# A transformer prompt kernel: the start-up sequence of the first token group rearranged, and a bias vector loaded late and element by element

## The chip, the cores and the metric

The kernel runs on one core of a Trainium2 chip. The metric is device time in microseconds (us). The profile's span runs from the first to the last instruction, and it is 1.7 to 2.2 us shorter than the time.

The core's engines go by the profile's names. PE does the matmuls and the transposes, and PEld is its loading of weights. DVE, ACT and POOL do the element-wise work. SP issues the DMAs; those that POOL issues are called software DMAs here. A DMA has landed when the trace shows that all its data has arrived. A *front* is the work before the first matmul on real weights.

## The reference

The input x has 2048 rows of 1024 columns, in bf16. Two layers are applied, with the same weights each time. Each layer does this:

```python
x = x + A(layernorm(x), wqkv, wo)          # 32 heads; each token attends to 8 tokens, 2 apart, to its left
x = x + B(layernorm(x), w1, b1, w2, b2)    # gelu_tanh(h @ w1 + b1) @ w2 + b2, 3584 hidden columns
```

In A, the logits of tokens before the start of the sequence get -1e9.

## The kernel before

The rows are worked on in four groups of 512 per layer. For each group PE computes Q, K and V, later the output projection (`gen_wo`), and then the two feed-forward products. DVE, ACT and POOL do all else beside it.

**The first loads.** SP issues all weight and x loads in one order. The first Q weight `wq` comes in four pieces of 512 KB, mixed with the first four x tiles of 256 KB each:

```python
load_x(0, 0, 2)
for k in range(0, KD, 2):
    load_wq_piece(wq_first[k // (KD // 2)], k)
    if k < 4:
        load_x(0, 2 + k // 2, 3 + k // 2)
```

The order is x0, x1, wq0, x2, wq1, x3, wq2, wq3. After these come x4 to x11 and then `wk`.

**The front.** Two token tiles are normalized and transposed on PE (cuts marked):

```python
xn0 = norm(0)
xn1 = norm(1)
transpose_on_pe(xn0, xa[0][:, 0, :, :], parts=[act.copy] * 4)
ps = transpose_bias()                      # b1, loaded as 28 rows by a software DMA on POOL
transpose_on_pe(xn1, xa[0][:, 1, :, :], parts=[vec.tensor_copy] * 2 + [act.copy] * 2)
warm_up(2)                                 # two matmuls that nobody reads
act.copy(b1T[:], ps[:])
# ... statistics of tiles 2 and 3
```

**The Q phase of group 0.** (K(0), or key(0), is the K phase after it.) The first products use those two tiles only. They run in four quarters over the contraction, one for each `wq` piece: 7 chunks x 2 matmuls of 128x256, so 14 matmuls a quarter:

```python
for kq in range(4 if n == 0 else 0):
    for c in range(7):
        first[c] = qkv_chunk(wq, c, xnT, first.get(c), kq * (KD // 4), (kq + 1) * (KD // 4), 0, 2)
        # at (2, 3) and (3, 4): transposes of token tiles 2 and 3
```

**The output projection.** It has two weight tiles. Chunks 0 to 3 use the first tile and chunks 4 to 7 the second:

```python
for tt in range(NTT):
    for dh in range(2):
        for c in range(NCH):
            mm(ps[:], lhsT=oT[:, c, tt * P:(tt + 1) * P], rhs=wts[c // 4][:, c % 4, ...], ...)
```

Of the kernel before, what the change touches and what calls it, by code (L numbers as in the profile page):

```python
# [9 lines left out]
ALU = mybir.AluOpType  # L10
# [7 lines left out]
def kernel(  # L18
# [134 lines left out]
    make_identity(nc, ident[:])  # L153
    mask = const.tile([P, W - 1, HALO], F32, name="mask")
    khalo = const.tile([P, NCH, HALO], BF16, name="khalo")
    vhalo = const.tile([P, NCH, HALO], BF16, name="vhalo")
    zhalo = const.tile([P, NCH, HALO], BF16, name="zhalo")
    b1T = const.tile([P, KF], F32, name="b1T")
    b2bc = const.tile([P, D], BF16, name="b2bc")
    mv_ahead = const.tile([P, NTT, 2], F32, name="mv_ahead")  # L160
    rstd_ahead = const.tile([P, NTT, 1], F32, name="rstd_ahead")

    def build_constants():
        pool.memset(zhalo[:], 0.0)
        pool.memset(mask[:], 0.0)
        first = smp.tile([H, W - 1, HALO], F32, name="z")
        pool.memset(first[:], 0.0)
        for w in range(W - 1):
            pool.memset(first[:, w, 0:HALO - DIL * w], -1e9)
        pool.dma_start(mask[0::NTT, :, :], first[:])  # L170

    b1_rows = attp.tile([KF, P], BF16, name="abc")

    pool.dma_start(b1_rows[:], B_b1.rearrange("(j p) -> j p", p=P))

    def load_b2():
        pool.dma_start(b2bc[:], B_b2.unsqueeze(0).to_broadcast([P, D]))

    def transpose_bias():
        ps = psum.tile([P, KF], BF16, name="acc", bufs=8)  # L180
        pe(nc.tensor.transpose(ps[:], b1_rows[:], ident[:KF, :KF]))  # L181
        return ps


    def ln_stats(t, mv=None, rstd=None):
        stats = lnp.tile([P, 2, 6], F32, name="stats")
# [7 lines left out]
        pool.tensor_tensor(out=rstd[:], in0=rstd[:], in1=mhalf[:], op=ALU.pow)  # L194
        return mv, rstd

    def ln_stats_ahead(g):
        junk = lnp.tile([P, D], BF16, name="xn", bufs=3)
        for tt in range(NTT):
            t, mean, var = g * NTT + tt, mv_ahead[:, tt, 0:1], mv_ahead[:, tt, 1:2]  # L200
            less = lnp.tile([P, 1], F32, name="less")
            act.activation(junk[:], x[t][:], ACT.Identity, scale=-1.0 / D, accum_out=less[:])
            act.activation(junk[:], x[t][:], ACT.Square, bias=less[:], accum_out=var)
            pool.tensor_scalar(out=mean, in0=less[:], scalar1=-1.0, scalar2=None, op0=ALU.mult)
            rstd = rstd_ahead[:, tt, :]
            pool.tensor_scalar(out=rstd, in0=var, scalar1=1.0 / D, scalar2=EPS, op0=ALU.mult, op1=ALU.add)
            pool.tensor_tensor(out=rstd, in0=rstd, in1=mhalf[:], op=ALU.pow)

    def ln_norm(t, mv, rstd, xn=None):
        if xn is None:  # L210
# [1 line left out]
        vec.tensor_scalar(out=xn[:], in0=x[t][:], scalar1=mv[:, 0:1], scalar2=rstd[:], op0=ALU.subtract, op1=ALU.mult)  # L212
        return xn

    def transpose_on_pe(xn, out, parts=None):
        pst = psum.tile([P, KD, P], BF16, name="acc", bufs=8)
        for k in range(KD):
            pe(nc.tensor.transpose(pst[:, k, :], xn[:, k * P:(k + 1) * P], ident[:]))  # L218
        parts = parts or [act.copy]
        n = KD // len(parts)  # L220
        for h, copy in enumerate(parts):
            copy(out[:, h * n:(h + 1) * n, :], pst[:, h * n:(h + 1) * n, :])

    last_transpose = [None]

# [7 lines left out]
    def ln_first():  # L233

        xa[0] = new_xnT()
        vec.on = act.on = True
        mvs = {}
        stds = {}

        def stats(tt):  # L240
            st6 = lnp.tile([P, 2, 6], F32, name="stats")
            for h in range(2):
                vec.bn_stats(st6[:, h, :], x[tt][:, h * HALF:(h + 1) * HALF])
            mvs[tt] = lnp.tile([P, 2], F32, name="mv")
            vec.bn_aggr(mvs[tt][:], st6[:])
            stds[tt] = lnp.tile([P, 1], F32, name="std")
            act.activation(stds[tt][:], mvs[tt][:, 1:2], ACT.Sqrt, bias=eps_t[:])

        def norm(tt):
            rstd = lnp.tile([P, 1], F32, name="rstd")  # L250
            vec.reciprocal(rstd[:], stds[tt][:])
            return ln_norm(tt, mvs[tt], rstd)

        stats(0)
        stats(1)
        xn0 = norm(0)
        xn1 = norm(1)
        transpose_on_pe(xn0, xa[0][:, 0, :, :], parts=[act.copy] * 4)
        ps = transpose_bias()
        transpose_on_pe(xn1, xa[0][:, 1, :, :], parts=[vec.tensor_copy] * 2 + [act.copy] * 2)  # L260
        warm_up(2)
        act.copy(b1T[:], ps[:])
        stats(2)
        stats(3)
        for tt in range(2, 4):
            first_late.append((norm(tt), xa[0][:, tt, :, :]))
        vec.on = act.on = False
        act.hold()
# [38 lines left out]
    def gen_qkv(n, defer=False, qk_pool=None, v_late=False, qk_next=None, v_first=False, mix=0):  # L307
        g = n % NG
        xnT = xa.pop(n)
        s = st[n]  # L310
        s["prods"] = []
        qk_pool = qk_pool or attp
        if v_first:
            wv = load_qkv(2)
        wq = wq_first if n == 0 else load_qkv(0)
        if not v_first:
            wk = load_qkv(1)

        def values():
            vT = attp.tile([P, NCH, HALO + T], BF16, name="vT", bufs=2)  # L320
            s["vT"] = vT
            act.on = n > 2
            act.copy(vT[:, :, 0:HALO], (zhalo if g == 0 else vhalo)[:])
            act.on = False
            for c in range(NCH):
                ps = qkv_chunk(wv, c, xnT)
                act.copy(vT[:, c, HALO:], ps[:])
                yield
            if g + 1 < NG:
                act.copy(vhalo[:], vT[:, :, T:T + HALO])  # L330

        if v_first:
            yield from values()
            wk = load_qkv(1)
        if n == 0:
            early_tiles = ln_early((1, None), (2, qk_next))
            for _ in range(NTT):
                next(early_tiles)
            wv = load_qkv(2)
            for _ in early_tiles:  # L340
                pass
            load_x(3)
        qT = qk_pool.tile([P, NCH, T], BF16, name="qT")
        first = {}
        for kq in range(4 if n == 0 else 0):
            for c in range(7):
                first[c] = qkv_chunk(wq, c, xnT, first.get(c), kq * (KD // 4), (kq + 1) * (KD // 4), 0, 2)
                if (kq, c) == (2, 3):
                    transpose_on_pe(*first_late.pop(0))
                if (kq, c) == (3, 4):  # L350
                    for done in range(2):
                        act.copy(qT[:, done, 0:2 * P], first[done][:, 0:2 * P])
                    transpose_on_pe(*first_late.pop(0))
                    act.hold()
        if n == 0:
            first[7] = qkv_chunk(wq, 7, xnT, t0=0, t1=2)
        for c in list(first)[2:]:
            act.copy(qT[:, c, 0:2 * P], first[c][:, 0:2 * P])
        kT = qk_pool.tile([P, NCH, HALO + T], BF16, name="kT")
        s["qT"], s["kT"] = qT, kT  # L360
        act.on = n > 2
        act.copy(kT[:, :, 0:HALO], (zhalo if g == 0 else khalo)[:])
        act.on = False

        def query(c):
            t0 = 2 if n == 0 else 0
            ps = qkv_chunk(wq, c, xnT, t0=t0)
            act.copy(qT[:, c, t0 * P:], ps[:, t0 * P:])

        def key(c):  # L370
            ps = qkv_chunk(wk, c, xnT)
            act.copy(kT[:, c, HALO:], ps[:])
            if not defer:
                new_prod(n, c)

        ahead = mix or NCH
        turns = [(query, c) for c in range(ahead)]
        for c in range(NCH):
            turns.append((key, c))
            if ahead + c < NCH:  # L380
                turns.append((query, ahead + c))
        for i, (chunk, c) in enumerate(turns):
            if i == NCH and n > 0 and not v_late and not v_first:
                wv = load_qkv(2)
            chunk(c)
            yield
        if g + 1 < NG:
            act.copy(khalo[:], kT[:, :, T:T + HALO])
        if not v_first:
            if v_late:  # L390
                wv = load_qkv(2)
            yield from values()
# [170 lines left out]
    def ln_early(*groups):  # L563
# [5 lines left out]
            tiles += [(n * NTT + tt, xns[:, tt, :], xa[n][:, tt, :, :]) for tt in range(NTT)]  # L569
        vec.on = True  # L570
        ahead = ln_stats(tiles[0][0])
        for i, (t, xn, xT) in enumerate(tiles):
            mv_rstd = ahead
            if i + 1 < len(tiles):
# [3 lines left out]
            if i + 1 == len(tiles):  # L578
                vec.on = False
            yield  # L580

    def stage(gen, count=None, sides=()):

# [21 lines left out]
    pool.on = True  # L605
    warm_up(14)
    ln_first()
    build_constants()
    with tc.tile_pool(name="early", bufs=1) as early:
        load_x(1)  # L610
        load_x(2)
        stage(gen_qkv(0, qk_next=early), sides=at(14, load_b2))
        q1 = gen_qkv(1, defer=True, qk_pool=early, mix=NCH // 2)
        stage(q1, sides=at(0, gather, 0) + at(11, between, 0, 1) + at(11, hold) + each(av, 0, 12, 1))
        q2 = gen_qkv(2, defer=True)
        stage(q2, 18)
        hold()
        stage(gen_wo(0))
        hold()
# [53 lines left out]
```

## Time and profile before

| | before |
|---|---|
| median before the prediction, 3 runs | 1231.02 us (1230.63 to 1231.93) |
| span of the profiled run | 1229.1 us |
| PE busy | 1221.3 us, 99% |
| first matmul on real weights | 8.95 us |

The page of the kernel before gives the busy time of each engine, the granted PE clock in 40 slices (9 is full) and the shares of the chain that ended last:

```profile
span 1229.1 us, 13953 instructions
PE 1221.3 (99%) x5723; PEld 632.7 (51%) x5773; DVE 864.2 (70%) x918; ACT 315.1 (26%) x507; POOL 105.2 (9%) x209
...
PEclk9999999999999999999999999999999999999999
...
PE 99%; DVE 0%; issue 0%; DMA 0%
```

PE is the limit almost everywhere. A change can gain only where PE does not yet work, or where it waits. The timeline of the kernel before shows the front. Its columns are start, duration, engine, line, operation, what is written from what, shape, count, and in brackets the idle time before it and what ended that:

```profile
3.60 1.29 DVE L92 BATCH_NORM_STATS2 stats<-x 128x6 f32<-128x512 bf16 x2 [2.67 <-DMA x<-in_A_x_dram]
...
7.19 0.62 PE L218 MATMUL acc<-ident,xn 128*128 128x128 bf16 x8 [1.09 <-DVE xn L92]
...
7.24 0.55 DVE L92 TENSOR_SCALAR xn<-x,mv,rstd 128x1024 bf16<-128x1024 bf16 x1
...
7.74 0.18 PE L181 MATMUL acc<-ident,abc 28*128 28x28 bf16 x1
7.85 1.90 ACT L92 COPY xnT<-acc 128x256 bf16<-128x256 bf16 x6 [1.00 <-PE acc L218]
...
7.86 0.62 PE L218 MATMUL acc<-ident,xn 128*128 128x128 bf16 x8
...
8.31 0.59 PE L117 MATMUL acc<-big 128*128 128x512 bf16 x2
8.52 0.49 DVE L92 COPY xnT<-acc 128x256 bf16<-128x256 bf16 x2 [0.73 <-PE acc L218]
...
8.95 4.12 PE L117 MATMUL acc<-xnT,wt 128*128 128x256 bf16 x36
```

Everything hangs on x0's landing at 3.57 us. The statistics start at 3.60, and the first real matmul comes 5.35 us after them. The last 0.6 us before that matmul go to two matmuls that nobody reads, while the copies finish.

One other place matters, the start of the first output projection:

```profile
124.02 6.19 PE L117 MATMUL acc<-wt,oT 128*128 128x512 bf16 x26
124.19 0.75 DVE L92 TENSOR_TENSOR oT<-big 128x512 bf16<-128x512 bf16 x2
...
125.08 4.84 PEld L117 LDWEIGHTS <-oT 128*128 128x128 bf16 x23 [0.32 <-DVE oT L92]
```

The single starts show one matmul 415 ns after the one before it, where 216 is usual. So 0.2 us are lost here.

### The profile page before, as it was taken

How to read it: one execution, taken by the hardware profiler on the slowest of the kernel's cores; microseconds unless marked ns; L12 is line 12 of the kernel's file. 1: busy time of each engine (PE TensorE's matmuls, PEld its weight loads, DVE VectorE, ACT ScalarE, POOL GpSimd, SP SyncE). 2: the span in 40 equal slices, each digit the busy share in tenths (PEclk: the TensorE clock that was granted, in tenths of full speed). 3: DMA queues.
4: the chain of work that ended last, by engine and by line, in shares of the span. 5: the costliest groups of instructions: out<-in, count | busy, mean ns of one | idle time of the engine just before them, and what ended most of it. 6: DMA issues, size and time to landing. Idle time of an engine off the chain costs nothing.

```text
span 1229.1 us, 13953 instructions
## 1 busy us (share of the span) xinstructions
PE 1221.3 (99%) x5723; PEld 632.7 (51%) x5773; DVE 864.2 (70%) x918; ACT 315.1 (26%) x507; POOL 105.2 (9%) x209
## 2 busy tenths in 40 slices
PE   9999999999999999999999999999999999999998
PEld 7666544456444564446544465444654444444444
DVE  8999896998997999375993759937599797011001
ACT  4343253014410144202441024410244001400310
POOL 3010015010101101100001000010000002000000
PEclk9999999999999999999999999999999999999999
DMA  9954674756648745856557565576664558446441
GB/s 299 293 205 154 178 238 153 201 171 206 215 133 239 188 151 167 235 169 181 155 160 233 171 171 175 155 222 202 171 199 145 189 195 203 155 160 195 154 136 52
DMA packets 220031, 226.64 MB, mean 184 GB/s; under 512 B 68194, under 2 KB 187136, under 8 KB 217920
## 3 DMA queue, kind: packets, MB, share of 16 engines
q1 hardware_dynamic: 214704, 208.69, 56.9%
q0 software_dynamic: 5264, 17.06, 3.6%
q8 instruction: 45, 0.74, 0.2%
q14 instruction: 18, 0.15, 0.0%
HBM read 189.01 MB, written 4.19 MB: 157 GB/s over the span
## 4 chain that ended last, share of the span: by engine, by line
PE 99%; DVE 0%; issue 0%; DMA 0%
PE acc L117 99%; DMA x<-in_A_x_dram 0%; DVE stats L92 0%; PE acc L218 0%; DVE xn L92 0%; DVE x L92 0%; DVE mv L92 0%; PE acc L181 0%; DVE rstd L92 0%
## 5 line engine op out<-in xcount | busy, mean ns | idle before, releaser
L117 PE MATMUL acc<-xnT,wt 128*128 128x512 bf16 (+1 forms) x3392 | 720.3, 375 | 0.1
L117 PEld LDWEIGHTS <-wt 128*128 128x128 bf16 x3392 | 400.8, 119 | 318.0 <-issue 0.5
L117 PE MATMUL acc<-wt,hT 128*128 128x512 bf16 (+1 forms) x1780 | 386.0, 376 | 2.1
L117 PEld LDWEIGHTS <-hT 128*128 128x128 bf16 x1820 | 178.1, 98 | 209.0
L92 DVE TENSOR_TENSOR big<-big 128x1024 bf16<-128x1024 bf16 (+2 forms) x184 | 244.7, 1358 | 2.2
L92 ACT ACTIVATE hT<-acc,b1T 128x512 bf16<-128x512 f32 x224 | 152.1, 687 | 325.1 <-PE acc L117 325.0
L92 DVE TENSOR_TENSOR big<-qT,kT 128x4096 bf16<-128x4096 bf16 x64 | 143.8, 2284 | 36.4 <-ACT kT L92 35.9
L92 DVE TENSOR_TENSOR tmp<-acc,b2bc 128x512 f32<-128x512 f32 x56 | 38.6, 689 | 161.6 <-PE acc L117 158.5
L92 DVE TENSOR_TENSOR big<-abc,vT 128x4096 bf16<-128x4096 bf16 x64 | 144.6, 2284 | 9.8 <-DMA abc<-a 7.4
L92 ACT CAST qT<-acc 128x512 bf16<-128x512 f32 (+1 forms) x72 | 38.2, 543 | 277.6 <-PE acc L117 277.6
L117 PE MATMUL acc<-wt,oT 128*128 128x512 bf16 x440 | 97.6, 379 | 0.5
L92 DVE BATCH_NORM_STATS2 stats<-x 128x6 f32<-128x512 bf16 x120 | 79.9, 680 | 3.7 <-DMA x<-in_A_x_dram 2.7
L117 PEld LDWEIGHTS <-oT 128*128 128x128 bf16 x448 | 43.8, 98 | 53.0 <-DVE oT L92 0.3
L92 DVE TENSOR_TENSOR x<-acc,big 128x512 bf16<-128x512 f32 (+1 forms) x9 | 5.7, 632 | 90.1 <-PE acc L117 90.0
L92 ACT CAST vT<-acc 128x512 bf16<-128x512 f32 x64 | 37.4, 585 | 100.9 <-PE acc L117 100.8
L92 POOL TENSOR_TENSOR rstd<-mv,eps_t 128x1 f32<-128x1 f32 x56 | 17.4, 311 | 527.5 <-DVE mv L92 527.5
L92 ACT CAST kT<-acc 128x512 bf16<-128x512 f32 x64 | 37.3, 585 | 68.7 <-PE acc L117 68.7
L92 DVE TENSOR_TENSOR x<-acc,x 128x512 bf16<-128x512 f32 x64 | 43.0, 672 | 4.9 <-PE acc L117 4.4
L92 DVE TENSOR_SCALAR xn<-x,mv,rstd 128x1024 bf16<-128x1024 bf16 x52 | 28.4, 546 | 19.9 <-POOL rstd L92 19.5
L92 DVE TENSOR_TENSOR x<-tmp,x 128x512 bf16<-128x512 f32 x56 | 38.6, 689 | 1.4
L92 POOL DMA_DIRECT2D big<-big x24 | 13.3, 563 | 212.8 <-DVE big L92 212.8
L92 POOL TENSOR_TENSOR rstd<-rstd,mhalf 128x1 f32<-128x1 f32 x56 | 30.9, 551 | 4.4
(63 smaller groups left out, 259.4 us busy)
## 6 DMA issues: line engine op xcount, KB each, us to landing
wt<-in_B_w_dram SPq DMA_DIRECT2D x56, 1024.0 KB, 5.8
wt<-in_B_w_dram SPq DMA_DIRECT2D x64, 896.0 KB, 4.9
wt<-in_A_wqkv_dram SPq DMA_DIRECT2D x46, 1024.0 KB, 5.7
wt<-in_A_wo_dram SPq DMA_DIRECT2D x16, 1024.0 KB, 5.3
abc<-a POOLq DMA_DIRECT2D x32, 256.0 KB, 4.7
big<-big POOLq DMA_DIRECT2D x24, 256.0 KB, 3.8
x<-in_A_x_dram SPq DMA_DIRECT2D x16, 256.0 KB, 5.7
out_dram<-x SPq DMA_DIRECT2D x31, 128.0 KB, 1.8
```

The source lines that it names most:

```text
L92: inst = f(*args, **kwargs)
L117: return pe(nc.tensor.matmul(*args, **kwargs))
```

## The change

The intent is a shorter front, and no software DMA while the first Q products run. The diff, cut to its core:

```diff
-    b1_rows = attp.tile([KF, P], BF16, name="abc")
-    pool.dma_start(b1_rows[:], B_b1.rearrange("(j p) -> j p", p=P))
+    def load_b1(q):                                    # element by element, straight into b1T
+        js = slice(q * (KF // 4), (q + 1) * (KF // 4))
+        pool.dma_start(b1T[:, js], B_b1.rearrange("(j p) -> p j", p=P)[:, js])
...
-        xn1 = norm(1)
-        transpose_on_pe(xn0, xa[0][:, 0, :, :], parts=[act.copy] * 4)
-        ps = transpose_bias()
-        transpose_on_pe(xn1, xa[0][:, 1, :, :], parts=[vec.tensor_copy] * 2 + [act.copy] * 2)
-        warm_up(2)
-        act.copy(b1T[:], ps[:])
+        xn1 = norm(1, (0, 2 * P, D))                   # normalized as 256 and 768 columns
+        transpose_on_pe(xn0, xa[0][:, 0, :, :], [(0, 2, act.copy), (2, 8, act.copy)])
+        transpose_on_pe(xn1, xa[0][:, 1, :, :], [(0, 2, vec.tensor_copy)])
+        transpose_on_pe(xn1, xa[0][:, 1, :, :], [(2, 8, act.copy)])
...
-        load_x(2)                                      # in the main program, before the first stage
...
         if n == 0:
+            load_x(2)                                  # x8 to x11: now behind wk, not ahead of it
             early_tiles = ln_early((1, None), (2, qk_next))
...
+        on_act = tiles[-2:]                            # in ln_early: tiles x10 and x11 are left out;
+        tiles = tiles[:-2]                             # ACT takes their statistics, DVE norms them later
...
-        stage(gen_qkv(0, qk_next=early), sides=at(14, load_b2))
+        stage(gen_qkv(0, qk_next=early), sides=at(9, ln_stats_ahead, 2, NTT - 2) + at(14, pool.dma_start, mask[0::NTT, :, :], first[:]) + at(11, ln_end) + at(14, load_b2))
...
-        stage(q2, 18)
+        stage(q2, 18, sides=each(lambda n, q: load_b1(q), 2, 4, 4, 0, 4))
```

The rest moves small halo copies (K and V of one group's last 14 tokens, to which the next group's first tokens attend) from ACT to POOL or drops them.

More of the change, by code (lines that the diff above doesn't have):

```diff
@@ L155 @@
     khalo = const.tile([P, NCH, HALO], BF16, name="khalo")
-    vhalo = const.tile([P, NCH, HALO], BF16, name="vhalo")
-    zhalo = const.tile([P, NCH, HALO], BF16, name="zhalo")
     b1T = const.tile([P, KF], F32, name="b1T")
@@ L163, in build_constants @@
     def build_constants():
-        pool.memset(zhalo[:], 0.0)
         pool.memset(mask[:], 0.0)
@@ L169, in build_constants @@
             pool.memset(first[:, w, 0:HALO - DIL * w], -1e9)
-        pool.dma_start(mask[0::NTT, :, :], first[:])
-    b1_rows = attp.tile([KF, P], BF16, name="abc")
-    pool.dma_start(b1_rows[:], B_b1.rearrange("(j p) -> j p", p=P))
+        return first
+    def load_b1(q):
+        js = slice(q * (KF // 4), (q + 1) * (KF // 4))
+        pool.dma_start(b1T[:, js], B_b1.rearrange("(j p) -> p j", p=P)[:, js])
     def load_b2():
         pool.dma_start(b2bc[:], B_b2.unsqueeze(0).to_broadcast([P, D]))
-    def transpose_bias():
-        ps = psum.tile([P, KF], BF16, name="acc", bufs=8)
-        pe(nc.tensor.transpose(ps[:], b1_rows[:], ident[:KF, :KF]))
-        return ps
     def ln_stats(t, mv=None, rstd=None):
@@ L195, in ln_stats, with ln_stats_ahead @@
         return mv, rstd
-    def ln_stats_ahead(g):
+    def ln_stats_ahead(g, t0=0):
+        act.on = g == 2
         junk = lnp.tile([P, D], BF16, name="xn", bufs=3)
-        for tt in range(NTT):
+        for tt in range(t0, NTT):
             t, mean, var = g * NTT + tt, mv_ahead[:, tt, 0:1], mv_ahead[:, tt, 1:2]
@@ L207, in ln_stats_ahead @@
             pool.tensor_tensor(out=rstd, in0=rstd, in1=mhalf[:], op=ALU.pow)
+        act.on = False
     def ln_norm(t, mv, rstd, xn=None):
@@ L213, in ln_norm, with transpose_on_pe @@
         return xn
-    def transpose_on_pe(xn, out, parts=None):
+    def transpose_on_pe(xn, out, parts):
         pst = psum.tile([P, KD, P], BF16, name="acc", bufs=8)
-        for k in range(KD):
+        for k in range(parts[0][0], parts[-1][1]):
             pe(nc.tensor.transpose(pst[:, k, :], xn[:, k * P:(k + 1) * P], ident[:]))
-        parts = parts or [act.copy]
-        n = KD // len(parts)
-        for h, copy in enumerate(parts):
-            copy(out[:, h * n:(h + 1) * n, :], pst[:, h * n:(h + 1) * n, :])
+        for k0, k1, copy in parts:
+            copy(out[:, k0:k1, :], pst[:, k0:k1, :])
     last_transpose = [None]
@@ L247, in stats, with norm @@
             act.activation(stds[tt][:], mvs[tt][:, 1:2], ACT.Sqrt, bias=eps_t[:])
-        def norm(tt):
+        def norm(tt, bounds=(0, D)):
             rstd = lnp.tile([P, 1], F32, name="rstd")
             vec.reciprocal(rstd[:], stds[tt][:])
-            return ln_norm(tt, mvs[tt], rstd)
+            xn = lnp.tile([P, D], BF16, name="xn", bufs=3)
+            for lo, hi in zip(bounds[:-1], bounds[1:]):
+                vec.tensor_scalar(out=xn[:, lo:hi], in0=x[tt][:, lo:hi], scalar1=mvs[tt][:, 0:1], scalar2=rstd[:],
+                                  op0=ALU.subtract, op1=ALU.mult)
+            return xn
         stats(0)
@@ L322, in values @@
             act.on = n > 2
-            act.copy(vT[:, :, 0:HALO], (zhalo if g == 0 else vhalo)[:])
+            if g == 0:
+                pool.memset(vT[:, :, 0:HALO], 0.0)
+            else:
+                (act.copy if n > 1 else pool.tensor_copy)(vT[:, :, 0:HALO], st[n - 1]["vT"][:, :, T:T + HALO])
             act.on = False
@@ L328, in values @@
                 yield
-            if g + 1 < NG:
-                act.copy(vhalo[:], vT[:, :, T:T + HALO])
         if v_first:
@@ L348, in gen_qkv @@
                 if (kq, c) == (2, 3):
-                    transpose_on_pe(*first_late.pop(0))
+                    transpose_on_pe(*first_late.pop(0), [(0, KD, act.copy)])
                 if (kq, c) == (3, 4):
@@ L352, in gen_qkv @@
                         act.copy(qT[:, done, 0:2 * P], first[done][:, 0:2 * P])
-                    transpose_on_pe(*first_late.pop(0))
+                    transpose_on_pe(*first_late.pop(0), [(0, KD, act.copy)])
                     act.hold()
@@ L361, in gen_qkv @@
         act.on = n > 2
-        act.copy(kT[:, :, 0:HALO], (zhalo if g == 0 else khalo)[:])
+        if g == 0:
+            pool.memset(kT[:, :, 0:HALO], 0.0)
+        else:
+            (act.copy if n > 1 else pool.tensor_copy)(kT[:, :, 0:HALO], st[n - 1]["kT"][:, :, T:T + HALO] if n < 3 else khalo[:])
         act.on = False
@@ L386, in gen_qkv @@
             yield
-        if g + 1 < NG:
+        if g + 1 < NG and n > 1:
             act.copy(khalo[:], kT[:, :, T:T + HALO])
@@ L580, in ln_early, with ln_end @@
             yield
+        ln_rest.append(on_act)
+    ln_rest = []
+    def ln_end():
+        vec.on = True
+        for tt, (t, xn, xT) in zip((NTT - 2, NTT - 1), ln_rest.pop()):
+            ln_norm(t, mv_ahead[:, tt, :], rstd_ahead[:, tt, :], xn)
+            sp.dma_start_transpose(xT, xn.rearrange("s (k p) -> s k p", p=P))
+        vec.on = False
     def stage(gen, count=None, sides=()):
@@ L607 @@
     ln_first()
-    build_constants()
+    first = build_constants()
     with tc.tile_pool(name="early", bufs=1) as early:
         load_x(1)
-        load_x(2)
-        stage(gen_qkv(0, qk_next=early), sides=at(14, load_b2))
+        stage(gen_qkv(0, qk_next=early), sides=at(9, ln_stats_ahead, 2, NTT - 2) + at(14, pool.dma_start, mask[0::NTT, :, :], first[:]) + at(11, ln_end) + at(14, load_b2))
         q1 = gen_qkv(1, defer=True, qk_pool=early, mix=NCH // 2)
```

## The prediction

> **What bounds the kernel now.** The PE. The page gives PE 99% of a 1229.1 us span, granted clock 1.00, and the chain of waits is 98.8% matmuls. Following matmul starts in the timeline, the 128x512 form starts every 216 ns and the 128x256 form every 109 ns from 8.95 us to the end, apart from regularly missing records. I find only two places where the PE is not at its cadence: before 8.95 us, and about 0.2 us near 124.8 us, where the first output projection waits for the last oT (the timeline shows the wait on oT; its DVE add ends at 124.94). After the last matmul some 3 us of output remain. The Trainium skill, page "TensorE: Matmul & The Clock Gate", gives N/2.4 GHz + 2.5 ns start to start when warm, 215.7 ns at N=512; the trace's 216 agrees. So no matmul can be made shorter by this change; only the front and that one wait can be.
>
> **The front.** Before: xn1 (0.55 us) ends at 7.79, its eight transposes at 8.48, the bias transpose takes 0.12 of PE's chain, two warm-up matmuls occupy PE 8.31-8.91, first real matmul 8.95. After: xn1 is normalized in pieces of 256 and 768 columns, the first two transposes have their own PSUM tile and DVE copies them at once; ACT copies 256 then 768 and 768 columns. From the timeline's durations (transpose every 56 ns, DVE copy about 0.25, ACT copy 0.32 for 256 and, by interpolation to 1.01 for 1024, about 0.79 for 768) I estimate the first real matmul at 8.3-8.4. But the second quarter needs ACT's third copy at about 9.8, and the first quarter takes 14 x 0.109 = 1.53, so there is no slack: up to 0.1 us may be lost there. Net about 0.55 us. Weights allow it: the wq pieces land at 6.71, 8.96, 10.81, 12.16, needed at about 8.4, 9.9, 11.4, 13.4.
>
> **What moves without time.** wk goes ahead of x8-x11: key(0) begins at about 23.5 and wk should land near 20-21 (before: 23.86, only 0.2 us before its use). x8 then lands near 21 rather than 17.6, so DVE waits 1-2 us there; PE does not. DVE loses two statistics (2 x 1.45 us), given to ACT in K(0), where ACT has 1.14 us idle per 1.73 us chunk. DVE's product chain starts at about 25.9 rather than 28.6, pays the two deferred norms (1.05) later, and is then held by kT(1) evictions, so it should be 0.8-1.5 us earlier through to oT. PE is 0.55 earlier; oT's 0.2 us wait should go. Halo copies leave ACT, off the path. The element-wise b1 loads follow the a-spread on POOL, so they issue close together near 86-90 us, not spread over the stage; 3,584 tiny elements slow the wk/wv loads of group 2 a few us, but those have about 10 us of slack.
>
> **Sum.** -0.55 (front) -0.2 (oT) = about -0.75 us, nothing in the 1,100 us after. 1231.0 becomes 1230.3 us, range 1229.3 to 1231.4, of which part is run-to-run spread (1230.63 to 1231.93 before). Chances: faster by over 2% 0.003, within 2% 0.99, slower 0.007.
>
> **What would show it.** Timeline: first 128x256 matmul at 8.3-8.45; second quarter without or with under 0.1 us of gap; no PE gap at key(0); no wait on oT near 124; the rest of PE shifted by one constant; b1T issues bunched near 87 us with landing well before the first gelu (139).
>
> **What would make it wrong.** The first transposes' copy waiting for all eight, leaving the first matmul near 8.7; a wq piece landing late, so that the front's gain is returned at the next quarter; x8's late landing or wv(0) (before: landed 36.69 for use at 37.9) stalling PE; element-wise b1 choking the queues for over 10 us; DVE not staying ahead, so that oT still waits.

## The result and the profile after

| | before | after |
|---|---|---|
| median, 6 runs each | 1230.87 us | 1230.57 us |
| range | 1230.55 to 1232.79 | 1230.13 to 1231.18 |
| span of the profiled run | 1229.1 us | 1228.4 us |
| first real matmul | 8.95 us | 8.26 us |
| PE's start-to-start at the first output projection's gap | 415 ns | 374 ns |

The ratio is 0.9995, 95% interval 0.9982 to 1.0008. A ratio is the mean time of one kernel's fast runs over that of the other's of the same rounds, so it is not quite the ratio of the medians. The two profiled spans differ by 0.7 us, near the prediction's sum of 0.75. The medians differ by 0.30 us and the means by 0.65 (two of the six runs before were at 1231.93 and 1232.79). The interval of the ratio reaches from 2.2 us less to 1.0 us more, so the times alone do not settle how large the gain is, or that there is one.

The page of the changed kernel:

```profile
span 1228.4 us, 13955 instructions
PE 1221.6 (99%) x5720; PEld 632.7 (52%) x5770; DVE 861.5 (70%) x912; ACT 315.6 (26%) x497; POOL 120.9 (10%) x219
...
PE 99%; DVE 0%; issue 0%; DMA 0%
```

The timeline of the changed kernel's front:

```profile
3.46 1.29 DVE L92 BATCH_NORM_STATS2 stats<-x 128x6 f32<-128x512 bf16 x2 [2.52 <-DMA x<-in_A_x_dram]
...
7.05 1.35 PE L211 MATMUL acc<-ident,xn 128*128 128x128 bf16 x16
7.10 0.73 DVE L92 TENSOR_SCALAR xn<-x,mv,rstd 128x256 bf16<-128x256 bf16 x2
7.70 1.78 ACT L92 COPY xnT<-acc 128x256 bf16<-128x256 bf16 x3 [0.99 <-PE acc L211]
7.82 0.29 DVE L92 COPY xnT<-acc 128x256 bf16<-128x256 bf16 x1
...
8.26 4.15 PE L117 MATMUL acc<-xnT,wt 128*128 128x256 bf16 x36
```

The first real matmul comes 4.80 us after the first statistics, where it was 5.35. That is 0.55 us of real gain. The other 0.14 us of the 0.69 is x0's landing at 3.43 instead of 3.57, which no edit here aims at. In the eleven other traces it landed between 3.42 and 3.90.

Later lines of the changed kernel's timeline:

```profile
21.85 1.29 DVE L92 BATCH_NORM_STATS2 stats<-x 128x6 f32<-128x512 bf16 x2 [1.50 <-DMA x<-in_A_x_dram]
...
26.82 4.49 DVE L92 TENSOR_TENSOR big<-qT,kT 128x4096 bf16<-128x4096 bf16 x2
...
87.82 3.76 POOL L92 DMA_DIRECT2D b1T<-in_B_b_dram  x4
...
123.17 0.75 DVE L92 TENSOR_TENSOR oT<-big 128x512 bf16<-128x512 bf16 x2
...
123.34 7.01 PE L117 MATMUL acc<-wt,oT 128*128 128x512 bf16 x30
...
124.36 5.71 PEld L117 LDWEIGHTS <-oT 128*128 128x128 bf16 x27 [0.28 <-issue]
```

DVE waits 1.5 us for x8. The four b1 loads are issued back to back. oT is done 1.0 us earlier than before (123.93 against 124.94), and yet 0.16 us of the gap at the projection stays. The difference of the matmul starts of the two traces is 0.69 us at the first matmul, 0.67 from 12 us on and 0.715 from 125 us to the end. So in this pair of traces nothing else happened.

Two questions are left. What ends the wait at the projection, if not oT? And why do the medians show less than the profiled pair? The changed kernel's own runs hint at an answer: their spans are 1228.4, 1228.4, 1228.4, 1229.1, 1229.3 and 1229.4.

### The profile page after: what moved, and what is told of

The parts are those of the page before. It is cut to its first block, busy times and chain, and to the rows that moved or that the text cites. A ratio compares the mean times of both kernels' runs of the same rounds, so it can differ in the third digit from the quotient of the medians.

```text
span 1228.4 us, 13955 instructions
## 1 busy us (share of the span) xinstructions
PE 1221.6 (99%) x5720; PEld 632.7 (52%) x5770; DVE 861.5 (70%) x912; ACT 315.6 (26%) x497; POOL 120.9 (10%) x219
## 3 DMA queue, kind: packets, MB, share of 16 engines
q0 software_dynamic: 8880, 17.07, 4.2%
## 4 chain that ended last, share of the span: by engine, by line
PE 99%; DVE 0%; issue 0%; DMA 0%
PE acc L117 99%; DMA x<-in_A_x_dram 0%; DVE stats L92 0%; PE acc L211 0%; DVE xn L92 0%; DVE x L92 0%; DVE mv L92 0%; DVE rstd L92 0%
## 5 line engine op out<-in xcount | busy, mean ns | idle before, releaser
L92 DVE BATCH_NORM_STATS2 stats<-x 128x6 f32<-128x512 bf16 x116 | 77.4, 681 | 6.0 <-DMA x<-in_A_x_dram 5.0
L92 DVE TENSOR_SCALAR xn<-x,mv,rstd 128x1024 bf16<-128x1024 bf16 (+2 forms) x53 | 28.5, 540 | 20.1 <-POOL rstd L92 19.9
```

What stands on the lines that cost most here:

```text
L92: inst = f(*args, **kwargs)
```

## The experiments

Eleven runs were made, of nine new kernels and of two once more, and all gave the reference's result. `wo_split`, `before_wo_split`, `old_order` and `front_only` ran on chip 13; `early_b1`, `dve_stats`, `x3_later` and `better` on chip 6; `after_again`, `x3_again` and `sw_early` on chip 9. Landing times come from the trace's record of each DMA.

### The second half of the first output projection's weight in two DMAs

The same edit was made on the changed kernel (`wo_split`) and on the kernel before (`before_wo_split`):

```diff
-            sp.dma_start(wt[:], wo_v[:, h * (NCH // 2):(h + 1) * (NCH // 2), :])
+            cuts = (0, 4) if n or h == 0 else (0, 2, 4)
+            for lo, hi in zip(cuts[:-1], cuts[1:]):
+                sp.dma_start(wt[:, lo:hi, :], wo_v[:, h * (NCH // 2) + lo:h * (NCH // 2) + hi, :])
```

> The changed kernel with one edit: the second half of the first output-projection weight (n = 0, h = 1) is loaded as two DMAs, chunks 4-5 and 6-7. Theory W: the 0.16 us PE gap that is left at 123.99 us waits for this weight's landing at 124.32, not for oT (done at 123.92). Then the first piece lands about 1.5 to 2 us earlier, the gap disappears (matmul to matmul under 240 ns, before 374) and every later matmul is 0.15 us earlier; span 1228.2 if the front repeats. Rival O, my prediction: the wait is on oT. Then the gap stays at 0.15 us.

> The kernel before with the same split of the second half of the first output-projection weight. There the weight landed at 125.03, oT was done at 124.94 and PE went on at 125.08, having been due at 124.88. Theory W: the weight ended the wait, but oT was only 0.1 us behind it, so the gap shrinks from 0.2 us to about 0.1 us and is then on oT. Rival O: oT alone held it; the gap stays 0.2 us.

In `wo_split` the 0.16 us at chunk 4 are gone, and 0.03 us remain before chunk 6. In `before_wo_split` the gap moved from the fifth matmul (chunk 4) to the seventh (chunk 6), with its size unchanged (418 ns from start to start). This is its weight-load timeline:

```profile
124.33 1.39 PEld L117 LDWEIGHTS <-oT 128*128 128x128 bf16 x7
126.04 4.84 PEld L117 LDWEIGHTS <-oT 128*128 128x128 bf16 x23 [0.32 <-issue]
```

The second part of the weight landed at 126.00, while oT had been done since 125.36. The gap follows the cut of the weight, so the weight ends the wait (theory W). That the gap would shrink to 0.1 us in the kernel before was wrong: the second part came 1.3 us after the first, and PE needs it 0.43 us after.

The original traces say the same if one counts matmuls. The gap in the kernel before sits between the fourth matmul (124.66) and the fifth (125.08). The fifth is chunk 4, the first to use the second weight tile, which landed at 125.03. The last oT chunk is used only by the eighth matmul, at 125.72.

All thirteen traces fit this. SP issues the second weight tile (or its first part) 4.12 us before the first matmul of the projection in each of them, and except in `better`, which reorders the matmuls, the fifth is due 0.86 us after the first. The landing took 5.27 us in `after_again` (0.32 us lost), 5.14 in the kernel before (0.20), 5.10 in the changed kernel (0.16), and 4.94 and 4.91 in `old_order` and `x3_again` (nothing lost). So an earlier oT could not have closed this gap, and the 0.04 us between the profiled pair is a matter of one landing.

As to time, `wo_split` had a median of 1230.15 us (ratio 0.9997) and `before_wo_split` 1231.86 (1.0010).

A surprise came with the `wo_split` profile: this run took 1232.15 us, with a span of 1230.4. Its PE timeline shows waits in the Q phase that the profiled changed kernel did not have, although the two programs are identical up to the output projection:

```profile
8.77 2.93 PE L117 MATMUL acc<-xnT,wt 128*128 128x256 bf16 x24
11.99 1.10 PE L117 MATMUL acc<-xnT,wt 128*128 128x256 bf16 x8 [0.30 <-DMA wt<-in_A_wqkv_dram]
```

The third `wq` piece landed at 11.95 here, and at 11.27 in the changed kernel's profile, where it was due at 11.35. This is a slack of 0.08 us against a spread of about 0.7. The second piece was late too (9.90), which makes 0.15 us of the 0.68 that this run lost in the Q phase. There was also a 1.2 us wait near 59 us for the K weight of group 1, which landed at 60.69 (57.24 in the changed kernel's profile). It was seen in this run and, smaller, in `early_b1` below.

### The old order of loads, and the front alone

`old_order` is the changed kernel with `load_x(2)` ahead of `wk` again:

```diff
-            load_x(2)
             early_tiles = ln_early((1, None), (2, qk_next))
...
         load_x(1)
+        load_x(2)
```

> The changed kernel with x8 to x11 loaded ahead of wk again, as in the kernel before. Theory: the order of the loads is what lets the front's gain be kept. wk's second half lands at about 23.9 us as before, while key(0) is due at about 23.36 (24.05 before less 0.69), so PE waits about 0.5 us in key(0) and 0.5 of the 0.69 us is returned; DVE no longer waits for x8. Rival: the order is a matter of DVE and ACT alone, PE shows no gap in 20 to 30 us and the shift of all matmuls stays 0.67 us.

Its weight-load timeline at the start of K(0):

```profile
19.95 4.50 PEld L117 LDWEIGHTS <-wt 128*128 128x128 bf16 x39
25.09 4.95 PEld L117 LDWEIGHTS <-wt 128*128 128x128 bf16 x24 [0.63 <-DMA wt<-in_A_wqkv_dram]
```

`wk`'s second half landed at 25.05, and PE lost 0.41 us (start-to-start excess). The kernel with the new order and the same late third piece (`wo_split`) has `wk` at 22.91 and no gap there. The same wait stands in one of the two traces of the old front. This is PE's timeline of `before_wo_split`:

```profile
19.81 4.96 PE L117 MATMUL acc<-xnT,wt 128*128 128x256 bf16 x40
25.00 5.18 PE L117 MATMUL acc<-xnT,wt 128*128 128x512 bf16 x23 [0.23 <-DMA wt<-in_A_wqkv_dram]
```

There `wk` landed at 24.95, and PE lost 0.46 us from start to start. In the first profile of the kernel before it landed at 23.86 and nothing was lost. So the old order had too little slack even for the old front. In all nine traces with the new order `wk` landed by 23.82, and no gap stands there. How much of the change's gain in time comes from it was not separated. The median was 1230.76 (ratio 0.9998).

`front_only` is the kernel before with only the front's edit. The bias transpose moved behind the late transposes, and the DMAs, the order of loads and the statistics stayed as they were:

```diff
-        transpose_on_pe(xn1, xa[0][:, 1, :, :], parts=[vec.tensor_copy] * 2 + [act.copy] * 2)
-        warm_up(2)
-        act.copy(b1T[:], ps[:])
+        transpose_on_pe(xn1, xa[0][:, 1, :, :], [(0, 2, vec.tensor_copy)])
+        transpose_on_pe(xn1, xa[0][:, 1, :, :], [(2, 8, act.copy)])
+        late_bias.append(lambda: act.copy(b1T[:], transpose_bias()[:]))
```

> The kernel before with the front's edit alone: xn1 in 256 and 768 columns, the split transposes and copies, no two warm-up matmuls, the bias transpose moved behind the late transposes; software DMAs, load order and statistics as before. Theory: measured from the first statistics on DVE, the first 128x256 matmul comes at 4.8 us as in the changed kernel (before 5.35), so the front's gain is the split's; then about 0.5 us is lost at key(0), which waits for wk landing at 23.9, so that the shift near 100 us is only 0.1 to 0.2 us. Rival, that the removal of the software DMAs makes the front faster: the first matmul stays at about 5.2 us or more after the statistics, or a weight piece lands late and a gap shows in the first four quarters.

The first matmul came 4.81 us after the statistics, so the 0.55 us belong to the front's edit as a whole (split copies, no warm-up matmuls, the bias transpose out of the way) and not to the removed DMAs. Its parts were not tried one by one. The loss at key(0) did not show. The third `wq` piece landed at 11.93, and 0.57 us were lost in the Q phase already, so that PE reached key(0) late and `wk` (24.32) was in time. After that quarter its matmuls stood where those of the kernel before stand (0.01 us earlier), and behind the moved bias transpose, which the changed kernel does not have, 0.25 us later, from 16 us on. The gain was all gone. The median was 1231.12 (ratio 1.0002).

### Software DMA in the Q phase

`early_b1` issues the four element-wise b1 loads first on POOL:

```diff
+    for q in range(4):
+        load_b1(q)
...
-        stage(q2, 18, sides=each(lambda n, q: load_b1(q), 2, 4, 4, 0, 4))
+        stage(q2, 18)
```

> The changed kernel with the four element-wise b1 loads issued first on POOL, so that they run during the first weight pieces (what the change's title avoids). Theory: software DMA is not what sets the landing of the wq pieces; the runs so far show them early (third piece at about 11.3 us) or late (11.95) with and without the two small software DMAs. 3,584 tiny elements are more than those two had, so I expect at most 0.5 us later pieces, the third at 11.3 to 12.4, and a span of 1228.4 to 1229.9. Rival, that software DMA in the Q phase is the harm that the change removes: the third piece lands more than 1 us later than 11.95 and the front's gaps add up to over 1.5 us, span over 1230.3.

The landing is given in the DMA view of its first 30 us (KB each, median us from issue to landing), and the PE timeline shows what followed:

```profile
b1T<-in_B_b_dram POOLq DMA_DIRECT2D x4, 3.5 KB, 16.6
...
10.37 1.75 PE L117 MATMUL acc<-xnT,wt 128*128 128x256 bf16 x14 [0.17 <-DMA wt<-in_A_wqkv_dram]
12.75 0.66 PE L117 MATMUL acc<-xnT,wt 128*128 128x256 bf16 x4 [0.63 <-DMA wt<-in_A_wqkv_dram]
```

The third piece landed at 12.70, 0.75 us after the latest of the other runs, and the front lost 1.25 us, 0.39 of it on the second piece. Another 0.60 us were lost near 60 us. The spans were 1229.6 to 1230.3 and the median 1231.86 (ratio 1.0007). Both expectations missed: more harm than mine, less than the rival's. All five times (1231.37 to 1232.12) lie above all eleven of the changed kernel (at most 1231.18), though in other rounds. Element-wise software DMA does cost the Q phase time here, and placing it late is right.

`sw_early` puts back only the two small software DMAs of the kernel before:

```diff
+    b1_rows = attp.tile([KF, P], BF16, name="abc")
+    pool.dma_start(b1_rows[:], B_b1.rearrange("(j p) -> j p", p=P))
...
+        pool.dma_start(mask[0::NTT, :, :], first[:])       # at once, not at step 14
```

> The changed kernel with the two small software DMAs of the kernel before put back at the start (28 rows of b1, here not used, and the mask), all else as changed. Theory: 20 KB in 64 packets cost the wq pieces nothing that shows; the third piece lands at 11.3 or 11.95 as in the changed kernel, the spans lie in the same two groups, 1228.4 and 1229.2. Rival, the title's: software DMA in the Q phase costs time; the third piece lands after 12.2 and every span is above 1229.5.

The third piece landed at 11.70, within the range of the runs without them. The spans were 1228.3, 1228.4, 1228.7, 1229.5 and 1229.6, and the median 1230.47, against 1230.45 for the changed kernel in the same rounds. These two small DMAs cost nothing that shows.

### The statistics of x10 and x11 back on DVE

```diff
-        on_act = tiles[-2:]
-        tiles = tiles[:-2]
...
-        stage(gen_qkv(0, qk_next=early), sides=at(9, ln_stats_ahead, 2, NTT - 2) + ... + at(11, ln_end) + at(14, load_b2))
+        stage(gen_qkv(0, qk_next=early), sides=... + at(14, load_b2))
```

> The changed kernel with the statistics and normalization of x10 and x11 back on DVE inside the early tiles. x10 lands at 23.2 us, so DVE starts its products about 3.3 us later than in the changed kernel (26.8), less the 1.05 us of the two norms that it no longer pays later. Theory: DVE is behind PE at the first output projection only by its margin there; last oT was done at 123.93 and its first use (the eighth matmul) came at 125.2, so 1.3 us of slack; of the delay of 2.2 us, PE then waits about 1 us near 125 us, now on oT. Rival: DVE is held elsewhere (by kT of group 1 or the abc landing) and catches up; then no gap on oT and the time is that of the changed kernel.

It was much slower than either theory said: 1235.85 us, ratio 1.0039 (1.0027 to 1.0052). The loss is not at oT but near 52 us. This is its PE timeline, and then one window (from:to, its length, PE's busy time and matmuls, the granted clock, the DMA share, GB/s):

```profile
52.05 1.08 PE L117 MATMUL acc<-xnT,wt 128*128 128x512 bf16 x4 [0.62 <-ACT vT L92]
54.77 5.52 PE L117 MATMUL acc<-xnT,wt 128*128 128x512 bf16 x17 [1.63 <-DMA wt<-in_A_wqkv_dram]
...
55.00:58.20 3.20, 3.20 (x9) 0.51 1.04 386
```

PE waits for the Q weight of group 1, whose halves landed at 52.01 and 54.72 (45.40 and 49.09 in the changed kernel). The label "ACT vT" of the first row misleads, as the one on oT did: the PEld row of the same moment names the weight. SP issued the first of these weights at 44.71, where it was 37.88. After the waits PE ran at half clock for 3.41 us, 9 matmuls in that window.

Both theories fell. What SP did before these loads is in its timeline, first of `dve_stats`, then of the changed kernel and of the kernel before:

```profile
27.82 14.74 SPq L92 DMA_TRANSPOSE xnT<-qT  x4
...
27.68 8.06 SPq L92 DMA_TRANSPOSE xnT<-qT  x2
...
27.54 11.69 SPq L92 DMA_TRANSPOSE xnT<-qT  x4
```

With the statistics in the early tiles, all four DMA transposes of group 2's x stand ahead of these weights in SP's queue. With two of the tiles left to ACT, two of the four stand behind them. That is the gain of handing over the statistics as far as the traces show it. The queue's order alone does not explain the loss, though: the kernel before has the same four transposes ahead, and its weights, issued at 41.38, came in time.

The transposes did not wait for DVE: the four tiles were normalized by 25.71, 27.56, 29.41 and 30.66, and SP began their transposes at 27.82, 31.72, 36.06 and 41.30. It was SP's issuing that took long: 3.80, 4.25, 5.14 and 1.26 us, against 4.65, 4.25, 1.26 and 1.26 in the kernel before. What held up the third is open. The edit also put the software DMAs of the mask and of b2 (issued at 30.16 and 30.87, landed at 38.76 and 41.74) beside these transposes; in the changed kernel they are issued near 41 us. No edit separates the two.

### The fourth x tile behind the third weight piece

If the lost gain is the late third piece, then 256 KB less ahead of that piece must help. `x3_later` does this, and DVE normalizes tile 2 before it takes tile 3's statistics:

```diff
-        if k < 4:
-            load_x(0, 2 + k // 2, 3 + k // 2)
+        if k in (0, 4):
+            load_x(0, 2 + k // 4, 3 + k // 4)
...
-        stats(2)
-        stats(3)
         for tt in range(2, 4):
+            stats(tt)
             first_late.append((norm(tt), xa[0][:, tt, :, :]))
```

> The changed kernel with one move: the fourth x tile is loaded behind the third wq piece instead of ahead of it, and DVE normalizes the third tile before it takes the fourth's statistics. Theory Q: in about half of the runs the wq pieces land 0.67 us late and the front's gain is lost because PE waits about 0.5 us for the third piece (due 11.35 us, landing 11.95; in the profile of the change 11.27). Then this kernel has the third piece at 10.6 (early runs) or 11.3 (late runs), no gap there in either, and the spans of its runs bunch at 1228.3 to 1228.7 instead of 1228.4 or 1229.3. Rival: the two groups of spans come from something else (the clock's start, the end); then they stay two, 0.8 us apart.

The third piece landed at 10.49 us. The PE timeline of `x3_later` has all 36 matmuls up to the late transposes in one row, without a wait:

```profile
8.38 4.13 PE L117 MATMUL acc<-xnT,wt 128*128 128x256 bf16 x36
12.34 0.61 PE L211 MATMUL acc<-ident,xn 128*128 128x128 bf16 x8
```

Its five spans were 1228.2 to 1228.5, the median 1230.12 and the ratio 0.9993. To see whether that was luck, the changed kernel (`after_again`) and this one (`x3_again`) ran once more in the same rounds, with no edit.

> The changed kernel once more, on the same chip and in the same rounds as the next two. Theory Q: its runs fall into two groups of spans, about 1228.4 and 1229.2, and in the profiled one the third wq piece lands at 11.3 or earlier without a gap if the span is of the first group, or near 11.95 with about 0.5 us of gaps if it is of the second. Rival: one group, or no connection of the group with that landing.

> The kernel with the fourth x tile behind the third wq piece, once more. Theory Q: all spans within 1228.1 to 1228.6, mean 0.3 to 0.5 us below the changed kernel's in the same rounds. Rival, that its first five runs were early by chance: two groups here too.

| | spans of the five timed runs, us | median, ratio | third piece landed | lost in the Q phase after the first matmul |
|---|---|---|---|---|
| `after_again` | 1228.3, 1228.5, 1228.7, 1228.8, 1228.8 | 1230.45, 0.9995 | 11.51 | 0.24 us |
| `x3_again` | 1228.2, 1228.2, 1228.4, 1228.8, 1228.8 | 1230.19, 0.9995 | 10.91 | 0.06 us |

Here the theory did not hold as I had put it. There are not two groups but a continuous spread, and two runs of `x3_again` lie outside the range that I gave. The means of the times differ by 0.14 us (1230.41 against 1230.28), less than the spread. `x3_later` has the lowest median of all runs here (1230.12, with `wo_split` at 1230.15 and `x3_again` at 1230.19), but that it beats the changed kernel is not shown by times. What is shown by the traces is the link between landing and loss, in this order of landings (the loss is the sum of the start-to-start excesses up to 14.5 us):

| trace | third piece landed, us | lost, us |
|---|---|---|
| x3_later, better, dve_stats | 10.49, 10.63, 10.80 | 0 |
| x3_again | 10.91 | 0.06, elsewhere |
| the changed kernel, profiled | 11.27 | 0.02 |
| after_again | 11.51 | 0.24 |
| sw_early | 11.70 | 0.43 |
| front_only | 11.93 | 0.57 |
| old_order, wo_split | 11.95, 11.95 | 0.64, 0.68 |
| early_b1 | 12.70 | 1.25 |

All rows have the new front, and their first matmul is at 8.25 to 8.73. The rows with the same order of the first loads lie together on one chip (11.93 to 11.95 on chip 13, 11.51 and 11.70 on chip 9), so how much of the spread is between chips and how much between runs of one chip was not separated. The edit does not explain all of it: `front_only` issues the same DMAs as the kernel before up to the first Q piece, which landed at 7.81 there and at 6.71 in the first profile. In the kernel before, the third piece is due 0.67 us later: it landed at 10.81 in the first profile and at 11.37 in `before_wo_split`, and neither shows a gap there.

In `after_again` the gap at the output projection shows its releaser more plainly. PE's row and PEld's row name two different ones:

```profile
124.77 2.53 PE L117 MATMUL acc<-wt,oT 128*128 128x512 bf16 x11 [0.16 <-DMA wt<-in_A_wo_dram]
...
124.78 6.14 PEld L117 LDWEIGHTS <-oT 128*128 128x128 bf16 x29 [0.44 <-DVE oT L92]
```

The weight landed at 124.73, and oT was done at 124.61. The label "DVE oT" on PEld is the one that misled the prediction.

### Two more edits on top

`better` is `x3_later` with x12 to x15 loaded behind the weights of group 2, and with chunks 0-3 of both halves of the first projection ahead of chunks 4-7:

```diff
-            load_x(3)
...
-        stage(q2, 18, sides=each(
+        stage(q2, 18, sides=at(0, load_x, 3) + each(
...
+            if n == 0 and tt == 0:                       # in gen_wo
+                for dh in range(2):
+                    ahead[dh] = acc_tile()
+                    project(tt, dh, ahead[dh], 0, NCH // 2)
```

> x3_later and two more: the fourth group's x is loaded behind the weights of group 2 instead of ahead of those of group 1, which takes 1 MB out of the queue between 36 and 40 us, and the first token tile's output projection does chunks 0-3 of both halves before 4-7 of both, so that the second weight half is needed 0.86 us later. Expected: no gap on wk near 59 us (1.2 us in one run of the split kernel), no gap at 124 us, wq of group 1 landing 2 to 3 us earlier; span 1228.1 to 1228.4, 0.15 us below x3_later, median time about 1230.0, and no run above 1231.

There is no gap from the first matmul on, and the profiled span is 1228.3. But the spans were 1228.2, 1228.2, 1228.3, 1228.7 and 1228.7 and the median 1230.41 (ratio 0.9996), not below `x3_later`. What makes the 1228.7 and 1228.8 in the last kernels was not found: those runs left no trace.

## Why the prediction was right, and where it was not

- **What bounds the kernel, and the size of the whole.** Right. PE stays at 99%, the time is the same within 2%, and the measured median of 1230.57 lies in the range 1229.3 to 1231.4. That says little for the mechanism: the range is 2.1 us wide, and the median of the kernel before, 1230.87, lies in it too.
- **The front, 0.55 us.** Right. From the first statistics, 5.35 became 4.80 us. The same 4.80 or 4.81 shows in all ten other traces with the new front. The first matmul was at 8.26, said was 8.3 to 8.4.
- **"Weights allow it."** This step failed. It compared due times with the landings of one profile. The third piece's landing was 10.81 in that one, and 11.27 to 11.95 in the traces with the same order of loads and no element-wise b1 (`dve_stats` again 10.80), while the new front makes it due at about 11.35. The due time of 11.4 was right; that a landing has a spread was not put into the sum. It costs 0 to 0.68 us in the traces with the new front, this order of the first loads and no element-wise b1 (0.02 and 0.24 in the two traces of the changed kernel itself). That the slower runs of the changed kernel, near 1229.2, lost their time there too is likely but not shown, since they left no trace. The medians moved by 0.30 instead of 0.75, the means by 0.65. The list of what could go wrong named it, but gave it no size.
- **"Up to 0.1 us may be lost" at ACT's third copy.** This did not show. In the profiled run no gap stands at the second quarter; where a gap did stand, it was on a DMA.
- **oT's 0.2 us.** The step "the first output projection waits for the last oT" failed. oT did come 1.0 us earlier, in the predicted 0.8 to 1.5, but the wait was for the second weight tile, which SP issues a fixed 4.12 us before PE's first matmul of the projection, however early oT is. The gain was 0.04 us, and in `after_again` the gap was 0.32.
- **The moves without time.** `wk` landed at 21.15 (said 20 to 21), x8 at 21.83 (21), DVE's wait was 1.50 us (1 to 2) and no gap stood at key(0). DVE's products started at 26.82, not 25.9. The b1 loads bunched at 87.8 to 91.6 and landed by 94.7. The next two weight loads took 0.5 us longer than before (5.7 and 7.5 us against 5.2 and 7.0), not a few us.
- **Which size was off.** The profiled pair gave 0.71 us, near the 0.75, but by partly other terms: 0.55 from the front, 0.14 from x0's landing, 0.02 given back in the third quarter and 0.04 at the projection.

## What to carry to other kernels

When work is pulled forward, compare its new due time with the landings of several traces, not of one: with 0.08 us of slack and 0.7 us of spread, part of the gain of the profiled pair is lost again in other runs (0.24 us in `after_again`). A wait that the profile puts down to one engine is settled by counting which operand is first used there, and an edit that moves that operand's boundary proves it. The order of a DMA queue is part of a kernel's schedule: in `dve_stats` four transposes ahead of a weight put its issue from 37.88 to 44.71 us.

## What the Trainium skill lacked or had wrong

- "TensorE: Matmul & The Clock Gate", table of the two states in Part 1: it has the clock fall after at least one idle window of about 3.4 us, and it does not say how much work such a window may hold. In `dve_stats` the clock was halved for 3.41 us (54.75 to 58.16 us), although PE had been busy for 1.19 of the 3.41 us before, with four matmuls from 52.05 us on, and the longest distance between two matmul starts was 2.01 us. So an unbroken pause of 3.4 us was not needed. The length of 3.41 us does agree with the page's window.
- "DMA: Bandwidth & Descriptors", Rules for kernel authors: it says that a non-contiguous last dimension becomes one descriptor per element. The packet count agrees: the software queue had 5,264 packets before and 8,880 after, 3,616 more, for 3,584 elements. The page has no number for what this costs beside other traffic. Here, at the start, four such loads of 3.5 KB took 16.6 us (median), and the third weight piece landed 0.75 us after the latest of the other runs. At 88 us they took 3.3 us.
- No page that I read has the spread of the first loads from run to run or from chip to chip. The same program's third 512 KB piece landed at 11.27 and at 11.51 us in two runs, and kernels with the same first loads had up to 11.95.
